# Another list order for a gated linear recurrence with an MLP mixer on one core

## The chip, the core and the metric

The kernel runs on one core of a Trainium2 chip. A core has five engines that run their own queues of instructions in order: PE (TensorE, the matmuls), DVE (VectorE), ACT (ScalarE), POOL (GpSimd) and SP (SyncE, which only issues transfers here). POOL and SP both issue transfers to the DMA engines. The metric is the device time of one execution in microseconds (us). The kernel before takes 167.32 us (median of 3 runs, 167.23 to 168.01).

## The reference

The inputs are q, k, v and f_logit of shape [4, 8, 768, 48] (batch, head, sequence, head width). A gated recurrence runs along the sequence; its output, with the 8 heads side by side as 384 channels, is the x of a mixer: two matmuls across the sequence (768 to 256 to 768) with a residual, then two across the channels (384 to 1536 to 384) with a residual.

```python
f = 1.0 / (1.0 + np.exp(-f_logit))
for t in range(S):
    state = f[:, :, t, :, None] * state + np.einsum('bhd,bhe->bhde', k[:, :, t], v[:, :, t])
    y[:, :, t] = np.einsum('bhd,bhde->bhe', q[:, :, t], state)

xt = x.transpose(0, 2, 1)
h = np.maximum(xt @ w_tok1, 0.0) @ w_tok2
u = x + h.transpose(0, 2, 1)
h2 = np.maximum(u @ w_ch1, 0.0) @ w_ch2
return (u + h2)
```

## The kernel before

The four batches b = 0 to 3 go one after the other, overlapped. A batch is cut into three pairs P = 0 to 2 of 256 positions; a pair is two chunks x = 0, 1 of 128 rows. For each pair the recurrence is done in a blocked form:

- Loads of f, k, q and v (L357), nearly all issued by POOL, to buffers that three batches share. ACT turns f_logit into the negative logarithm of the gate (L454, L457, L459), DVE or POOL adds neighbouring rows (`two`, L448), PE makes running sums with a triangular matrix (L479 for b0, L481 and L482 after it), DVE subtracts (`first`, L499), and ACT takes exponentials into `GG` (L502, L519).
- q and k are multiplied by `GG` into `qk` (L448, one instruction for each j of two, both on DVE except where b0 lets POOL do it), and then turned, so that the head width lies on the partitions. For b0 and b1 PE turns them (L546), and two copies move the result out of PSUM: `kT` (L436 on DVE or L434 on ACT) and the strided `qT`. For b2 and b3 two DMA transposes do it, issued by SP (L531): k straight to `kT`, q to `qJ`, from which POOL (L438) or ACT (L434) makes the strided copy `qT`.
- PE multiplies turned q and k into the scores (L581) and k with v into the parts of the state (L599). DVE masks the scores into `AmT` in four instructions (L624; some of b0's go through ACT and POOL, L619 and L621).
- The state is carried from chunk to chunk by DVE: for b0 it lies in PSUM and is multiplied by the gate of the chunk (L633, the rows `ps<-ps,glast`); later L636, L639 and L641. Each new state is copied to bf16 in two pieces (`state_bd`, L436, L434 or L438).
- PE makes the output of the pair: the earlier state's share (L657) and the masked scores' share (L665). Copies bring it to `x_nat` (fp32) and `x_bf` (bf16).

Then comes the mixer of the batch: tok1 (L709) and its relu `h1T` (L443, L445), tok2 (L725), the residual (L741), its bf16 copy `u_bf`, the turn of `u_bf` to `uT` (by PE for b0 and b1, L766; by two DMA transposes on SP for b2 and b3, L755), ch1 (L784) and its relu `zT` (ACT L443 or DVE L445), ch2 (L803), the last residual (L814) and the store (L702).

All of this is first only a list of operations with their needs. The tuple `ORDER` holds one number for each operation: four times its place in that list, plus which of its allowed engines takes it. `Plan.best` walks `ORDER`, gives each operation a planned start by its own table of costs, deals out the eight PSUM banks as it goes, and at the end sorts all operations by planned start; this is the order in which each engine gets its instructions. Where the plan leaves PE without work for more than 270 ns before 25.5 us, it puts filler matmuls there (L852, function `idle`), whose result nobody reads. The engines take no notice of the planned starts: they run their own queue in order and wait on semaphores.

The lines that choose the engine and place the fillers:

```python
op = self.ops[code // 4]
e = op.engine = op.engines[code % 4]
...
if e == PE and free[PE] < until and t - free[PE] > 270:
    n = int(t / 410) if not free[PE] else int((t - free[PE] - 50) / 215)
    fill = Op((PE,), 0.0, lambda n=n: idle(n), (), (), None, ("fill", n))
```

`idle(n)` issues n // 4 matmuls in fp32 and n % 4 in bf16, each over 512 columns.

Of the kernel before, what the change touches and what calls it, by code (L numbers as in the profile page):

```python
# [35 lines left out]
    884, 888, 920, 1368, 1372, 1264, 164, 168, 172, 1376, 1380, 1156, 1276, 1280, 1284, 1288, 1292, 1240, 1160,
    1400, 1404, 1388, 1384, 1204, 1392, 1208, 1296, 1312, 1412, 1324, 1408, 1300, 1308, 1528, 1304, 1532, 1128,
    956, 932, 1132, 1424, 1416, 924, 908, 936, 1428, 928, 960, 912, 1136, 1316, 1320, 1420, 1140, 1536, 948,
    952, 1540, 1432, 1436, 1440, 1444, 1448, 176, 180, 184, 628, 1396, 1456, 940, 1460, 1328, 945, 1560, 1544,
    1564, 1548, 1552, 2204, 1568, 1468, 1572, 1452, 1088, 1092, 1096, 1340, 1344, 1348, 1100, 1336, 2208, 1332,  # L40
    2228, 1464, 1472, 1584, 1364, 1352, 1588, 1356, 1108, 1576, 1112, 1116, 1580, 1484, 2232, 1592, 1596, 1600,
    1604, 632, 636, 640, 644, 1556, 1476, 1480, 1360, 2212, 1612, 1488, 1620, 1608, 1624, 1616, 1068, 1500,
    1504, 1716, 1720, 1508, 1072, 2236, 1496, 1492, 2216, 1516, 1512, 1640, 1644, 1744, 1628, 1632, 1636, 1648,
    1520, 1652, 2388, 1120, 2240, 2392, 1657, 648, 652, 656, 660, 1748, 1724, 1752, 1728, 1756, 1760, 1660,
    2260, 2248, 2264, 2244, 1764, 1732, 664, 668, 672, 1668, 1524, 2220, 1664, 2252, 1736, 1769, 1741, 2272,
    2268, 1168, 1172, 1772, 1776, 1144, 1104, 2284, 1784, 1788, 1780, 1792, 1796, 1808, 1800, 1804, 1812, 1816,
    2396, 1820, 1824, 1828, 1832, 1836, 1840, 1176, 2280, 1852, 1860, 1856, 1864, 1844, 1848, 1076, 1884, 2400,
    2224, 2408, 2424, 2404, 1888, 1868, 1876, 1892, 1900, 1872, 1880, 2552, 1956, 2412, 1960, 1904, 2420, 2428,
    1897, 1080, 2432, 1180, 2044, 2076, 1988, 2080, 2293, 2048, 1964, 1969, 2556, 2288, 1972, 2012, 2016, 1977,
    1992, 2004, 1908, 1913, 1996, 2008, 2000, 1672, 1676, 2276, 2296, 2300, 2304, 2308, 2312, 2256, 2444, 2436,  # L50
    2416, 2316, 2332, 2560, 2336, 1680, 2340, 1684, 2452, 1688, 1692, 1696, 1700, 2564, 2344, 2320, 2324, 2328,
    2568, 2052, 2056, 2060, 2068, 2036, 1924, 2020, 1916, 1948, 2572, 2584, 2588, 2592, 2596, 2576, 1928, 2072,
    1932, 1921, 2360, 2364, 2025, 2065, 2368, 2028, 1980, 1940, 2348, 1937, 3144, 2033, 2040, 3148, 3168, 1952,
    2376, 2440, 2184, 2188, 2448, 2381, 2385, 3172, 2372, 1944, 1984, 2352, 2356, 2456, 2460, 2464, 2468, 2472,
    3176, 3152, 3184, 2192, 2480, 2488, 3180, 2492, 2484, 2476, 3156, 3188, 3204, 3160, 2496, 2196, 2505, 2501,
    2104, 2608, 3192, 2617, 3200, 3208, 2084, 2108, 2612, 2112, 2116, 2088, 2508, 2512, 2124, 2604, 2092, 2096,
    2524, 2528, 3212, 2600, 2580, 1184, 3196, 2620, 2624, 2628, 2632, 2128, 2532, 1124, 1084, 3224, 3216, 2636,
    2652, 2648, 2640, 2644, 2540, 1704, 2517, 1708, 2521, 2656, 2665, 2536, 3164, 2544, 3492, 3328, 3332, 3496,
    2660, 2548, 2724, 2144, 2728, 2732, 2696, 2736, 2700, 2704, 2668, 2672, 3220, 2676, 2708, 2148, 2680, 2688,
# [826 lines left out]
```

## Time and profile before

| what | value |
|---|---|
| median of 3 runs (lowest, highest) | 167.32 us (167.23, 168.01) |
| the profiled execution's own time | 167.16 us |
| span of the profiled execution, first to last instruction | 165.5 us |
| mean granted TensorE clock | 0.996 |
| busy time PE, DVE, ACT, POOL | 157.5, 128.0, 108.0, 64.7 us |
| filler matmuls L852 | 8.8 us of PE's busy time, before about 25 us |

The profiled execution's time is 1.66 us more than its span; this part lies before the first and behind the last instruction. Busy times of PE count a matmul until its modelled end, so that neighbouring matmuls overlap in the table: the step from one start to the next is what a matmul costs in a full queue. A timeline row gives start, length, engine, line, operation, output and inputs with partitions by elements, the number of instructions in the row, and in brackets the idle time before it with what ended it.

### The profile page before, as it was taken

How to read it: one execution, taken by the hardware profiler on the slowest of the kernel's cores; microseconds unless marked ns; L12 is line 12 of the kernel's file. 1: busy time of each engine (PE TensorE's matmuls, PEld its weight loads, DVE VectorE, ACT ScalarE, POOL GpSimd, SP SyncE). 2: the span in 40 equal slices, each digit the busy share in tenths (PEclk: the TensorE clock that was granted, in tenths of full speed). 3: DMA queues.
4: the chain of work that ended last, by engine and by line, in shares of the span. 5: the costliest groups of instructions: out<-in, count | busy, mean ns of one | idle time of the engine just before them, and what ended most of it. 6: DMA issues, size and time to landing. Idle time of an engine off the chain costs nothing.

```text
span 165.5 us, 4987 instructions
## 1 busy us (share of the span) xinstructions
PE 157.5 (95%) x2050; PEld 100.8 (61%) x2050; DVE 128.0 (77%) x285; ACT 108.0 (65%) x229; POOL 64.7 (39%) x87
## 2 busy tenths in 40 slices
PE   7899998999999999999999999889999999999991
PEld 3286765566665765656666766546657656666561
DVE  6678994998999999999999999937989639271142
ACT  3888985887999999997999567085611422543000
POOL 7998979944876820004603416112122011000000
PEclk9999999999999999999999999999999999999998
DMA  5999999999999999706995991990640043300295
GB/s 121 223 177 171 202 210 241 184 223 210 219 225 222 248 242 210 163 6 128 108 180 135 145 144 34 127 240 1 130 144 6 0 79 80 83 0 0 96 338 190
DMA packets 68184, 24.34 MB, mean 147 GB/s; under 512 B 60897, under 2 KB 67297, under 8 KB 68161
## 3 DMA queue, kind: packets, MB, share of 16 engines
q0 software_dynamic: 41856, 13.77, 68.8%
q1 hardware_dynamic: 25776, 10.06, 29.5%
q8 instruction: 16, 0.26, 0.7%
q10 hardware_dynamic: 528, 0.20, 0.5%
q14 instruction: 8, 0.06, 0.1%
HBM read 25.17 MB, written 4.72 MB: 181 GB/s over the span
## 4 chain that ended last, share of the span: by engine, by line
PE 76%; DMA 4%; ACT 2%; DVE 2%; issue 0%; SPq 0%
PE ps L803 27%; PE ps L784 27%; PE ps L709 5%; DMA uT<-u_bf 4%; PE ps L725 3%; PE ps L665 3%; PE ps L581 3%; PE ps L657 3%; PE ps L546 2%; PE ps L766 1%; PE ps L599 1%; PE ps L481 1%; DVE x_nat L741 1%; DVE x_nat L814 1%; PE ps L482 1%; ACT u_bf L434 1%
## 5 line engine op out<-in xcount | busy, mean ns | idle before, releaser
L803 PE MATMUL ps<-w_ch,zT 128*128 128x384 bf16 (+2 forms) x300 | 52.6, 320 | 0.0
L784 PE MATMUL ps<-uT,w_ch 128*128 128x384 bf16 x288 | 49.6, 326 | 1.5 <-DMA uT<-u_bf 1.4
L784 PEld LDWEIGHTS <-w_ch 128*128 128x128 bf16 x288 | 27.6, 98 | 20.0 <-DMA uT<-u_bf 2.1
L803 PEld LDWEIGHTS <-zT 128*128 128x128 bf16 x300 | 28.0, 98 | 17.0 <-DVE zT L445 0.2
L443 ACT ACTIVATE zT<-ps 128x384 bf16<-128x384 f32 x57 | 25.6, 505 | 18.7 <-PE ps L784 18.4
L624 DVE TENSOR_TENSOR AmT<-ps,mask 128x512 bf16<-128x512 f32 x44 | 28.7, 684 | 1.6 <-PE ps L581 1.5
L445 DVE TENSOR_SCALAR zT<-ps 128x384 bf16<-128x384 f32 x39 | 20.2, 552 | 9.7 <-PE ps L784 6.0
L814 DVE TENSOR_TENSOR x_nat<-x_nat,ps 128x384 f32<-128x384 f32 (+2 forms) x25 | 13.0, 534 | 8.3 <-PE ps L803 8.1
L438 POOL CAST state_bd<-state 48x192 bf16<-48x192 f32 x15 | 5.6, 371 | 24.3 <-DVE state L641 23.6
L438 POOL COPY qT<-qJ 128x1024 bf16<-128x1024 bf16 x3 | 3.5, 1151 | 29.0 <-DMA qJ<-qk 24.6
L448 DVE TENSOR_TENSOR qk<-qk_sb,GG 128x768 bf16<-128x768 bf16 x22 | 12.0, 553 | 1.8 <-ACT GG L519 1.5
L741 DVE TENSOR_TENSOR x_nat<-x_nat,ps 128x384 f32<-128x384 f32 x21 | 10.4, 549 | 3.6 <-PE ps L725 3.6
L357 POOL DMA_DIRECT2D v_sb<-in_v_dram x12 | 10.7, 894 | 5.0 <-DMA w_ch<-in_moe_w_ch_dram 3.8
L519 ACT ACTIVATE GG<-first 128x384 bf16<-128x384 f32 x24 | 12.1, 524 | 0.1
L502 ACT ACTIVATE GG<-ps 128x384 bf16<-128x384 f32 x24 | 11.4, 486 | 0.6 <-PE ps L486 0.5
L434 ACT ACTIVATE x_nat<-ps 128x384 f32<-128x384 f32 x15 | 7.2, 487 | 6.8 <-PE ps L665 6.8
L357 POOL DMA_DIRECT2D qk_sb<-in_k_dram x12 | 10.9, 908 | 1.5 <-POOLq L870 0.8
L357 POOL DMA_DIRECT2D qk_sb<-in_q_dram x12 | 10.8, 900 | 0.8 <-DMA qk_sb<-in_q_dram 0.5
L709 PE MATMUL ps<-x_bf,w_tok 128*128 128x384 bf16 x48 | 10.3, 327 | 0.0
L434 ACT ACTIVATE u_bf<-x_nat 128x384 bf16<-128x384 f32 x13 | 6.3, 533 | 5.8 <-DVE x_nat L741 5.5
L852 PE MATMUL ps<-steady 128*128 128x512 f32 (+1 forms) x18 | 8.8, 595 | 1.0 <-DVE steady L372 1.0
L725 PE MATMUL ps<-h1T,w_tok 128*128 128x384 bf16 x48 | 9.4, 326 | 0.1
(88 smaller groups left out, 233.6 us busy)
## 6 DMA issues: line engine op xcount, KB each, us to landing
out_dram<-x_nat SPq DMA_DIRECT2D x23, 192.0 KB, 2.2
f_sb<-in_f_logit_dram POOLq DMA_DIRECT2D x9, 384.0 KB, 9.4
qk_sb<-in_k_dram POOLq DMA_DIRECT2D x12, 192.0 KB, 8.2
qk_sb<-in_q_dram POOLq DMA_DIRECT2D x12, 192.0 KB, 8.1
v_sb<-in_v_dram POOLq DMA_DIRECT2D x12, 192.0 KB, 8.7
w_ch<-in_moe_w_ch_dram POOLq DMA_DIRECT2D x2, 576.0 KB, 13.7
w_ch<-in_moe_w_ch_dram POOLq DMA_DIRECT2D x1, 1152.0 KB, 10.7
f_sb<-in_f_logit_dram SPq DMA_DIRECT2D x2, 384.0 KB, 5.6
```

Of the source, the lines that this page charges most:

```text
L357: lambda eng=eng, into=held(dst[i], P), of=runs(src, b, P): eng.dma_start(out=into, in_=of),
L434: nc.scalar.activation(out_, in_, AF.Copy, bias=0.0, scale=1.0)
L443: nc.scalar.activation(out_, in_, AF.Relu, bias=0.0, scale=1.0)
L445: nc.vector.tensor_scalar(out_, in_, 0.0, None, ALU.max)
L519: add(ACT, r, lambda n=n: nc.scalar.activation(GG[i][:, 0, n], first[i], AF.Exp, bias=0.0, scale=2.0 * n - 1.0), need=[("first", i)] + ([" ...
L624: add(DVE, r, lambda into=into, made=made, m4=m4: nc.vector.tensor_tensor(into, made(), m4, ALU.mult), need=masks, make=[("AmT", i, js, pa ...
L709: add(PE, rank("tok1", rt), lambda rt=rt, kt=kt, pm=pm: nc.tensor.matmul(banks[pm.at][:, 0:DM], lhsT=w_tok1[:, kt, rt * 128:(rt + 1) * 128 ...
L725: nc.tensor.matmul(banks[pm.at][:, 0:DM], lhsT=w_tok2[:, kt, tt * 128:(tt + 1) * 128], rhs=h1T[:, kt, :], start=(kt == 0 and not held), st ...
L741: nc.vector.tensor_tensor(to, un, banks[pm.at][:, 0:DM], ALU.add)
L784: nc.tensor.matmul(banks[pm.at][:, 0:384], lhsT=w[:, kt, c0:c0 + 128], rhs=uT[:, th, :, kt, :], start=(kt == 0), stop=(kt == 2))
L803: nc.tensor.matmul(banks[pm.at][:, 0:n1 - n0], lhsT=zT[:, kt, tt * 128:(tt + 1) * 128], rhs=w_ch2[:, kt, n0:n1], start=(kt == 0), stop=(kt ...
L814: add(DVE, rank("ch2", tt), lambda un=un, pm=pm, n=n1 - n0: nc.vector.tensor_tensor(un, un, banks[pm.at][:, 0:n], ALU.add), make=[("x_nat" ...
```

## The change

Only the numbers in `ORDER` change. The tuple has 1026 entries before and after, for the same operations, so the loads, matmuls, masks and copies are the same ones; what differs is the order of each engine's queue, which of the allowed engines takes some of the copies and products, the PSUM bank of some results, and the fillers that follow from the plan. The core of the diff, one line of each side:

```diff
@@ -21,61 +21,61 @@
 TURNED = 2
 NQ = 2
 ORDER = (
-    0, 4, 12, 16, 8, 20, 24, 28, 32, 188, 192, 196, 80, 88, 92, 96, 100, 357, 104, 108, 48, 36, 40, 44, 52, 56,
...
+    3780, 3801, 3956, 3884, 3844, 3960, 3817, 3904, 3848, 3785, 3924, 3928, 3864, 3804, 3825, 3932, 3892, 3876,
...
 )
```

Counted over the program, ACT gets 2 more activations (229 for 227), DVE 4 fewer relus (39 for 43), 3 more `state_bd` casts of b0 (5 for 2), 2 more products `qk` of b0 (24 for 22), one more `two` of b0 (12 for 11) and two `qT` copies out of PSUM that ACT had; POOL loses one `two` and two products `qk` of b0, and takes one more `qT` copy of a later batch. There are 5 fillers in fp32 as before, and 16 in bf16 where there were 8. Three places are shown, in the order in which the engines get the instructions. Numbers behind a name are buffers; `ps_4` and the like are PSUM banks; `qk0`, `qk1`, `AmT0`, `AmT1` alternate from pair to pair.

The first place is DVE's queue in the start-up, b0, from the products `qk` of pair 1 (`qk1`) on. Before, it reads:

```order
L448 TENSOR_TENSOR two0_76<-f_sb0_74 128x8x48
L448 TENSOR_TENSOR qk1_85<-qk_sb0_68,GG1_83 128x2x8x48
L633 TENSOR_TENSOR ps_2_123<-ps_2_123,glast0_94 128x192
L624 TENSOR_TENSOR AmT0_92<-ps_4_125,mask_116 128x512
L624 TENSOR_TENSOR AmT0_92<-ps_6_127,mask_116 128x512
L624 TENSOR_TENSOR AmT0_92<-ps_3_124,mask_116 128x512
L633 TENSOR_TENSOR ps_2_123<-ps_2_123,glast0_94 128x192
L499 TENSOR_TENSOR first0_80<-ps_0_121,f_sb0_74 128x384
L436 COPY kT1_89<-ps_4_125 128x1024
L633 TENSOR_TENSOR ps_2_123<-ps_2_123,glast1_95 128x192
L436 CAST state_bd2_103<-ps_2_123 48x4x48 x2
L448 TENSOR_TENSOR qk0_84<-qk_sb0_68,GG0_82 128x2x8x48
```

In the new order the same stretch is:

```order
L448 TENSOR_TENSOR qk1_85<-qk_sb0_68,GG1_83 128x2x8x48 x2
L436 CAST state_bd0_101<-ps_1_122 48x4x48 x2
L448 TENSOR_TENSOR two0_76<-f_sb0_74 128x8x48
L624 TENSOR_TENSOR AmT0_92<-ps_4_125,mask_116 128x512
L633 TENSOR_TENSOR ps_1_122<-ps_1_122,glast0_94 128x192
L624 TENSOR_TENSOR AmT0_92<-ps_3_124,mask_116 128x512
L436 CAST state_bd1_102<-ps_1_122 48x4x48
L624 TENSOR_TENSOR AmT0_92<-ps_6_127,mask_116 128x512
L499 TENSOR_TENSOR first0_80<-ps_5_126,f_sb0_74 128x384
L624 TENSOR_TENSOR AmT1_93<-ps_0_121,mask_116 128x512
L633 TENSOR_TENSOR ps_1_122<-ps_1_122,glast1_95 128x192
L436 CAST state_bd2_103<-ps_1_122 48x4x48 x2
```

Both products `qk` of pair 1 (`qk1`) are now DVE's, and further down both of pair 2 (`qk0`), where POOL had one of each; three more pieces of `state_bd` are DVE's; the copy `kT1` has gone to ACT, and just ahead of this stretch a `qT0` has come.

The second place is the end of the same start-up on DVE, up to the copies `x_bf` that feed tok1 of b0. Before:

```order
L624 TENSOR_TENSOR AmT1_93<-ps_1_122,mask_116 128x512
L436 COPY kT0_88<-ps_6_127 128x1024
L624 TENSOR_TENSOR AmT1_93<-ps_4_125,mask_116 128x512
L633 TENSOR_TENSOR ps_2_123<-ps_2_123,glast2_96 128x192
L624 TENSOR_TENSOR AmT0_92<-ps_0_121,mask_116 128x512
L624 TENSOR_TENSOR AmT0_92<-ps_6_127,mask_116 128x512
L624 TENSOR_TENSOR AmT0_92<-ps_4_125,mask_116 128x512
L436 COPY x_nat0_104<-ps_1_122 128x384
L436 CAST x_bf0_107<-ps_0_121 128x384
```

And in the new order:

```order
L624 TENSOR_TENSOR AmT1_93<-ps_2_123,mask_116 128x512
L436 COPY x_nat0_104<-ps_6_127 128x384
L436 COPY kT0_88<-ps_3_124 128x1024
L436 CAST x_bf0_107<-x_nat0_104 128x384
L624 TENSOR_TENSOR AmT0_92<-ps_0_121,mask_116 128x512
L624 TENSOR_TENSOR AmT0_92<-ps_3_124,mask_116 128x512
L624 TENSOR_TENSOR AmT0_92<-ps_6_127,mask_116 128x512
L633 TENSOR_TENSOR ps_1_122<-ps_1_122,glast2_96 128x192
L436 CAST x_bf0_107<-ps_4_125 128x384
```

The last multiplication of b0's state (`glast2`) stood ahead of the three masks of pair 2, and now stands behind them; `x_nat0`, `kT0` and one `x_bf0` stand ahead of them.

The third place is batch b2, where pair 2's `qk0` must be made before SP can issue its two transposes. On DVE, from the masks of pair 0 (`AmT0`) to these products, before:

```order
L624 TENSOR_TENSOR AmT0_92<-ps_0_121,mask_116 128x512
L636 TENSOR_TENSOR state_99<-ps_7_128,glast0_94 128x192
L499 TENSOR_TENSOR first0_80<-ps_6_127,f_sb0_74 128x384
L639 TENSOR_TENSOR tsum_100<-state_99,ps_3_124 128x192
L624 TENSOR_TENSOR AmT0_92<-ps_5_126,mask_116 128x512
L624 TENSOR_TENSOR AmT0_92<-ps_4_125,mask_116 128x512
L624 TENSOR_TENSOR AmT0_92<-ps_1_122,mask_116 128x512
L448 TENSOR_TENSOR qk0_84<-qk_sb2_70,GG0_82 128x2x8x48 x2
```

In the new order:

```order
L624 TENSOR_TENSOR AmT0_92<-ps_7_128,mask_116 128x512
L624 TENSOR_TENSOR AmT0_92<-ps_5_126,mask_116 128x512
L624 TENSOR_TENSOR AmT0_92<-ps_4_125,mask_116 128x512
L624 TENSOR_TENSOR AmT0_92<-ps_0_121,mask_116 128x512
L499 TENSOR_TENSOR first0_80<-ps_6_127,f_sb0_74 128x384
L814 TENSOR_TENSOR x_nat1_105<-x_nat1_105,ps_3_124 128x384
L448 TENSOR_TENSOR two1_77<-f_sb1_75 128x8x48
L448 TENSOR_TENSOR two0_76<-f_sb1_75 128x8x48
L636 TENSOR_TENSOR state_99<-ps_2_123,glast0_94 128x192
L639 TENSOR_TENSOR tsum_100<-state_99,ps_1_122 128x192
L448 TENSOR_TENSOR qk0_84<-qk_sb2_70,GG0_82 128x2x8x48 x2
```

Two sums `two` and one residual L814 have come in between the masks and the products. POOL's queue beside this, which issues the loads of b3 (buffers `sb0`, and `f_sb1`), read:

```order
L357 DMA f_sb1_75<-in_f_logit_dram 128x8x96
L438 COPY qT1_87<-qJ1_91 128x1024
L357 DMA qk_sb0_68<-in_k_dram 128x8x96
L357 DMA qk_sb0_68<-in_q_dram 128x8x96
L357 DMA v_sb0_71<-in_v_dram 128x8x96
L357 DMA f_sb1_75<-in_f_logit_dram 128x8x96
L438 CAST state_bd2_103<-state_99 48x4x48 x2
L357 DMA qk_sb0_68<-in_k_dram 128x8x96
L438 CAST state_bd0_101<-state_99 48x4x48
L357 DMA qk_sb0_68<-in_q_dram 128x8x96
```

and now reads:

```order
L357 DMA qk_sb0_68<-in_k_dram 128x8x96
L357 DMA qk_sb0_68<-in_q_dram 128x8x96
L438 COPY qT0_86<-qJ0_90 128x1024
L438 COPY qT1_87<-qJ1_91 128x1024
L438 CAST state_bd0_101<-state_99 48x4x48 x2
L357 DMA v_sb0_71<-in_v_dram 128x8x96
L357 DMA f_sb1_75<-in_f_logit_dram 128x8x96
L357 DMA qk_sb0_68<-in_k_dram 128x8x96
L438 CAST state_bd2_103<-state_99 48x4x48
L357 DMA qk_sb0_68<-in_q_dram 128x8x96
L438 CAST state_bd2_103<-state_99 48x4x48
L357 DMA v_sb0_71<-in_v_dram 128x8x96
```

Two loads (k and q of one pair) have moved ahead of the copies `qT`; v, f and k now stand behind the first two casts of b2's `state_bd`, and the last v of b3 follows the last q with one cast between them, where six POOL instructions stood between them before.

108 rows, old and new, of the table ORDER are left out of this document.

## The prediction, on record before the changed kernel ran

> **What bounds the kernel now.** I read the busy times and the chain of the page first, then PE's waits, then timelines of the places where the list differs.
>
> ```profile
> span 165.5 us, 4987 instructions
> PE 157.5 (95%) x2050; PEld 100.8 (61%) x2050; DVE 128.0 (77%) x285; ACT 108.0 (65%) x229; POOL 64.7 (39%) x87
> PE 76%; DMA 4%; ACT 2%; DVE 2%; issue 0%; SPq 0%
> ```
>
> PE is busy for 95% of the span and carries 76% of the chain. The same matmuls run after the change, so the time can move in two ways only: PE waits more or less in the start-up, or it waits more or less in a stall behind it. The waits of PE behind the start-up come down to one row:
>
> ```profile
> PE ps L784 <- DMA uT<-u_bf: 1.4, 2, 0.8
> ```
>
> The columns are total, times and longest: ch1 of b2 waits twice for the transposed `uT`, 1.4 us in all. That is all that a better list could take away in the later part; what a worse one can add has no such limit.
>
> **Term A, the start-up.** Before ch1 of b0 can run, the recurrence of b0 must be through, and DVE is its engine. The first rows are the load of q of pair 1 with its neighbour and their time to landing, then a row by stretch with the busy times of PE, PEld, DVE, ACT and POOL, then DVE's own rows.
>
> ```profile
> L357 POOL DMA_DIRECT2D qk_sb<-in_q_dram x1: 893/893/893, 5.3 to 5.3; - x1
> DMA to landing us min/median/max: 7.6/7.8/7.9
> 13.50:25.04 11.54, 10.61 (x270) 8.16 (x259) 10.84 (x23) 10.08 (x23) 9.94 (x10) 1.00 1.48 197
> 13.51 0.56 DVE L448 TENSOR_TENSOR two<-f_sb 128x384 f32<-128x384 f32 x1 [0.82 <-issue]
> 13.99 0.55 DVE L448 TENSOR_TENSOR qk<-qk_sb,GG 128x768 bf16<-128x768 bf16 x1
> 14.46 0.36 DVE L633 TENSOR_TENSOR ps<-ps,glast 128x192 f32<-128x192 f32 x1
> 14.72 1.88 DVE L624 TENSOR_TENSOR AmT<-ps,mask 128x512 bf16<-128x512 f32 x3
> 16.96 0.56 DVE L499 TENSOR_TENSOR first<-ps,f_sb 128x384 f32<-128x384 f32 x1
> 17.44 0.68 DVE L436 COPY kT<-ps 128x1024 bf16<-128x1024 bf16 x1
> 18.54 0.72 DVE L436 CAST state_bd<-ps 48x192 bf16<-48x192 f32 x2
> 22.47 0.36 DVE L633 TENSOR_TENSOR ps<-ps,glast 128x192 f32<-128x192 f32 x1
> 23.15 1.89 DVE L624 TENSOR_TENSOR AmT<-ps,mask 128x512 bf16<-128x512 f32 x3 [0.33 <-PE ps L581]
> 24.96 0.55 DVE L436 COPY x_nat<-ps 128x384 f32<-128x384 f32 x1
> 25.46 0.56 DVE L436 CAST x_bf<-ps 128x384 bf16<-128x384 f32 x1
> ```
>
> DVE is busy 10.84 of the 11.54 us to the end of the last mask of pair 2 at 25.04: it sets this stretch. From the rows its steps are, start to start or a little more: a product `qk` 0.48, a sum `two` 0.48, a mask 0.60 (three take 1.88), `first` and each 384-wide copy 0.48, `kT` 0.60 like the mask it nearly equals in length, a piece of `state_bd` 0.36, a multiplication of the state 0.36. The work that the new list puts on DVE cannot begin before q of pair 1 has landed, at 5.34 + 7.9 = 13.26 (the row starts at 5.3 in its rounding). From there to the last `glast2` multiplication stand 26 instructions: 4 `qk`, 4 copies and sums of 384 columns (`two`, `first`, `x_nat`, `x_bf`), 5 pieces of `state_bd`, 8 masks, 4 multiplications, 1 `kT`. By the steps: 4 x 0.48 + 4 x 0.48 + 5 x 0.36 + 8 x 0.60 + 4 x 0.36 + 0.60 = 12.48, so DVE is through at 25.74, 0.70 later than 25.04. Its last instruction is now the state's, from which the path runs on through ACT and PE:
>
> ```profile
> 24.18 0.66 ACT L434 ACTIVATE state_bd<-ps 48x192 bf16<-48x192 f32 x2 [0.42 <-PE ps L657]
> 26.03 0.34 PE L657 MATMUL ps<-state_bd,qT 128*128 128x96 bf16 x4
> 27.93 1.79 PE L725 MATMUL ps<-h1T,w_tok 128*128 128x384 bf16 x10
> ```
>
> Two `state_bd` casts on ACT take 0.66, with a wake on each side L657 starts at about 26.55 where it started at 26.03; from there the matmuls are the same down to tok2. So 0.5 later without any idle time on DVE, and 1.2 with the 0.70 of idle that the stretch has now. The program gives a bound further up: it has eight more bf16 fillers of 512 columns. Fillers stand only where the plan sees PE idle, one for each 215 ns by its own rule, so its list leaves PE 8 x 0.215 = 1.7 more without work in the start-up. They delay nothing by themselves, since they stand where PE waits anyway, but they say that the waits are longer. The lower end is 0: a state multiplication steps on by 0.26, not 0.36, where nothing waits for it, and four of these give back 0.4. I take 0.8, between 0.5 and 1.2.
>
> The products that POOL gives up cost it these rows:
>
> ```profile
> 7.10 1.03 POOL L448 TENSOR_TENSOR two<-f_sb 128x384 f32<-128x384 f32 x1
> 14.40 1.64 POOL L448 TENSOR_TENSOR qk<-qk_sb,GG 128x768 bf16<-128x768 bf16 x1
> ```
>
> POOL is freed of 1.03 + 2 x 1.64 = 4.3 us, while DVE pays 3 x 0.48; the 0.48s are in the sum above. POOL's gain is on no path, because what follows it there, the masks of L621, already waits for ACT. The `qT` copies that come to DVE have no row of that form; from below they cost 0.68 as `kT` of the same size, from above the 1.17 that ACT takes for a strided one (row below). Both lie ahead of 13.26, while DVE waits for q, so they cost nothing; without that cover they would add up to 2 x 1.17.
>
> **Term B, the transposes of pair 2 in b2.** SP, POOL, DVE and ACT now, with the landing times of L531 at 80.8 to 82.2, at 92.8 to 94.4, and over the whole program:
>
> ```profile
> 76.16 0.69 DVE L624 TENSOR_TENSOR AmT<-ps,mask 128x512 bf16<-128x512 f32 x1 [0.28 <-PE ps L581]
> 79.59 1.17 DVE L448 TENSOR_TENSOR qk<-qk_sb,GG 128x768 bf16<-128x768 bf16 x2
> 77.65 0.87 POOL L357 DMA_DIRECT2D qk_sb<-in_k_dram  x1
> 80.25 0.92 POOL L357 DMA_DIRECT2D f_sb<-in_f_logit_dram  x1
> 80.80 1.24 SPq L531 DMA_TRANSPOSE qJ<-qk  x1
> 82.13 3.60 SPq L531 DMA_TRANSPOSE kT<-qk  x1
> DMA to landing us min/median/max: 7.4/7.7/7.9
> DMA to landing us min/median/max: 6.8/7.2/7.6
> DMA to landing us min/median/max: 3.0/3.5/7.9
> 89.41 1.17 ACT L434 ACTIVATE qT<-qJ 128x1024 bf16<-128x1024 bf16 x1
> 92.03 0.64 PE L581 MATMUL ps<-qT,kT 48*64 48x128 bf16 x32
> ```
>
> A transpose that has the DMA engines to itself lands 3.0 after its issue, one issued behind loads needs 6.8 to 7.9. In the kernel before, four loads go out from 77.65 to 80.25 just ahead of the pair; it lands late, and nobody waits, because the scores are due 11.2 us after the issue.
>
> In the new list that room is smaller. PE's steps come from the chain:
>
> ```profile
> 84.96 0.57 PE ps L581 x32
> 85.53 0.25 PE ps L599 x32
> 86.22 5.20 PE ps L803 x32
> 91.42 0.17 PE ps L657 x4
> 91.59 0.51 PE ps L665 x32
> ```
>
> A matmul of 384 columns takes 5.20 / 32 = 0.1625. Counted in the new list, PE has 65 of them from the scores of pair 0 to those of pair 2 (32 of L803, 27 of L784, 2 of L709, 4 running sums): 10.56. With two scores at 0.57, two parts at 0.25, two outputs at 0.51 and 12 matmuls of L657 in fours at 0.17 this makes 13.73. In the old list the same count is 80 wide matmuls, and 8 of L657: 16.0. On DVE the road to the transposes is 4 masks 2.40, `first` 0.48, one L814 0.48, two sums `two` 0.96, L636 and L639 at 0.26 each, two `qk` 1.17: 6.0. With 0.5 from the start of the scores to the first mask, SP issues `qJ` 6.55 after the scores of pair 0, which leaves 13.73 - 6.55 = 7.2; less 1.25 for the `qT` copy with its wakes, `qJ` may take 5.95. `kT` goes out 1.33 later (80.80 to 82.13) and needs no copy: 5.9. Ahead of them POOL issues v, f and k, and q and v come just behind.
>
> The landing is the unknown. From below it is 3.0, and there is no stall. From above I take 7.9 and one more load's step of 0.9, 8.8, since two loads follow the transposes: a stall of 2.9. The rows nearest to the case are the four that landed behind loads, 7.9, 7.4, 7.6 and 6.8, mean 7.4: a stall of 7.4 - 5.9 = 1.5, which I take. While ACT's queue stands at that `qT` copy, relus of ch1 wait behind it and hold PSUM banks; between 0 and 0.6, I take 0.2.
>
> **Term C, the uT stall.** The first b2 transposes of `uT` and their landing:
>
> ```profile
> DMA to landing us min/median/max: 3.3/4.7/6.1
> ```
>
> One landed in 3.3, the other in 6.1 beside the load of v. That load now follows q with one cast between and is over long before. So the 1.4 of PE's wait goes: -1.4. If another transfer takes its place nothing is gained, so this term lies between -1.4 and 0; I take -1.4, because POOL's list has no load left then. What is late next is ch1's own bank, which zT frees.
>
> Edits with one answer: relus that go from DVE to ACT, bank numbers, and the order of fillers cost nothing, being covered by PE's full queue behind 25 us (ACT is busy 65%); if ACT were full there, two relus would cost PE up to 1 us. The tail from the last ch2 to the store has the same operations.
>
> **The sum.** 167.16 (span 165.5 and 1.66 around it) + 0.8 + 1.5 + 0.2 - 1.4 = 168.3. The profiled execution is 0.16 below the median of 167.32, so this is +0.6% against the median. Within 0.5% of 167.32, 166.5 to 168.15, is about what a measurement of this kernel can tell from no change.
>
> **Rivals.**
> - *The transposes get their share, and the time is no longer than before (R1).* They stand on SP's queue, the loads on POOL's; if both were served in turn, a transpose would take at most twice the 3.2 that lies between 3.0 and the median 3.5, so 6.4; the stall would be 0.5 and the time 167.16 + 0.8 + 0.5 - 1.4 = 167.1. If both land within 5.9 of their issue it is 166.6, and at 7.2 (a stall of 1.3) the sum passes the 0.5% line. For it speaks that a transpose alone lands in 3.0; against it that the four behind loads took 6.8 to 7.9, over the double. The Trainium skill, page "DMA: Bandwidth & Descriptors", section "Queues, rings and completion order", says that each DMA engine goes round the queue rows that have work, packet by packet; by that rule R1 would hold. The rows agree only in part, since they are longer than a fair share gives.
> - *The loads hold them (R2).* If q and v, issued behind, push the transposes to 8.8, the stall is 2.9 and ACT's queue adds 0.6: 167.16 + 0.8 + 2.9 + 0.6 - 1.4 = 170.1. For it: SP's `kT` at 82.13 took 3.60 for its issue alone, where `qJ` took 1.24, so it was held up there. Against: the old list had four loads just ahead, and still no transpose took over 7.9.
> - *The start-up is no later (R3).* POOL's 4.3 us less could let pair 1 and 2 start sooner, so that DVE's queue begins earlier than 13.26 + waits: A is 0 and the time 167.16 + 1.7 - 1.4 = 167.5. For it: DVE idles 0.70 now; against: that stretch has 23 instructions on DVE now, the new list 26 behind the landing of q, which it cannot move.
>
> **Chances.** The forecast case 0.46 (own range 167.5 to 169.2: 0.28 slower by over 0.5%, 0.18 within), R1 0.20 (0.09 faster, where term A also lies at its low end, 0.11 within), R2 0.22 (slower), R3 0.12 (0.03 faster, 0.07 within, 0.02 slower). Sum: faster 0.12, within 0.5% 0.36, slower 0.52. The range goes from R1's middle, 166.7, to just under R2's, 170.0, leaving about one in ten on each side.
>
> **What the changed profile would show.** A: L657 ahead of tok1 of b0 starts near 26.5 to 26.9, and the first tok2 near 28.7, not 27.93. B: PE's row L581 of pair 2 in b2 waits about 1.5 for `qT` or `kT`, and L531 lands over 6. C: the row `PE ps L784 <- DMA uT<-u_bf` is gone. The prediction is wrong if a wait shows that I have no term for, such as ch2 waiting for `zT` or scores of b1 or b3 waiting for their copies, or if B's landings come within 5.9.

## The result, and the profile after

The changed kernel takes 174.28 us (median of 4 runs, 173.13 to 175.10), the kernel before 167.27 us (median of 4): a ratio of 1.0409 with a 95% interval of 1.0360 to 1.0458. The prediction of 168.3 us (166.7 to 170.0) had the direction and missed the size by 6 us. The profiled execution took 173.54 us. Here and below a ratio and its interval leave out runs more than 1.5% above the fastest of their kernel, while medians and ranges hold every run.

The head of the page of the changed kernel, the chain by engine, and its three longest waits of PE behind the first microseconds:

```profile
span 171.8 us, 5005 instructions
PE 160.6 (93%) x2058; PEld 102.3 (60%) x2058; DVE 129.8 (76%) x285; ACT 108.3 (63%) x231; POOL 61.9 (36%) x85
PE 69%; DMA 8%; ACT 3%; DVE 2%; issue 1%; POOL 1%; DVEq 0%
...
PE ps L581 <- DMA kT<-qk: 3.2, 1, 3.2
PE ps L709 <- POOL AmT L621: 1.2, 1, 1.2
PE ps L665 <- issue: 1.2, 1, 1.2
```

The span is 6.3 us longer. PE's wait for `uT` (1.4 us before) is gone from the list. PE's timeline of the start-up shows two of the new waits:

```profile
14.57 0.64 PE L581 MATMUL ps<-qT,kT 48*64 48x128 bf16 x32
20.99 0.22 PE L665 MATMUL ps<-v_sb,AmT 64*128 64x48 bf16 x3 [1.16 <-issue]
27.04 0.81 PE L709 MATMUL ps<-x_bf,w_tok 128*128 128x384 bf16 x4 [1.25 <-POOL AmT L621]
30.74 1.95 PE L725 MATMUL ps<-h1T,w_tok 128*128 128x384 bf16 x11 [0.25 <-ACT h1T L443]
33.73 2.11 PE L784 MATMUL ps<-uT,w_ch 128*128 128x384 bf16 x12 [0.38 <-ACT uT L434]
```

The first scores of b0 start 1.50 later than before (13.07), tok2 2.81 later (27.93) and ch1 3.05 later (30.68). The third wait is that of b2: the transposes with POOL's loads ahead of them, the landing of the two, and the scores.

```profile
85.36 0.88 POOL L357 DMA_DIRECT2D v_sb<-in_v_dram  x1
87.11 0.89 POOL L357 DMA_DIRECT2D qk_sb<-in_k_dram  x1
85.88 1.25 SPq L531 DMA_TRANSPOSE qJ<-qk  x1
87.22 2.09 SPq L531 DMA_TRANSPOSE kT<-qk  x1
DMA to landing us min/median/max: 6.7/8.0/9.2
96.49 0.64 PE L581 MATMUL ps<-qT,kT 48*64 48x128 bf16 x32 [3.24 <-DMA kT<-qk]
```

Right behind it the granted clock of PE, the third number from the end of a row by stretch, is not 1.00:

```profile
96.00:98.00 2.00, 1.51 (x50) 1.15 (x51) 0.97 (x3) 0.80 (x3) 0.00 (x0) 0.78 1.87 157
98.00:100.00 2.00, 2.00 (x8) 0.97 (x7) 2.00 (x5) 0.49 (x1) 0.00 (x0) 0.50 0.04 3
100.00:102.00 2.00, 2.00 (x29) 1.22 (x28) 1.07 (x3) 1.20 (x3) 0.00 (x0) 0.87 0.10 22
```

At these shares PE loses 2.0 x (0.22 + 0.50 + 0.13) = 1.7 us; at half speed that is a stretch of 3.4 us. So the account of the span is 3.05 (start-up) + 3.24 (wait for `kT`) + 1.7 (clock) - 1.4 (`uT`) = 6.6, against 6.3 measured.

### The profile page after: what moved, and what is told of

The parts are those of the page before. It is cut to its first block, busy times and chain, and to the rows that moved or that the text cites. A ratio compares the mean times of both kernels' runs of the same rounds, so it can differ in the third digit from the quotient of the medians.

```text
span 171.8 us, 5005 instructions
## 1 busy us (share of the span) xinstructions
PE 160.6 (93%) x2058; PEld 102.3 (60%) x2058; DVE 129.8 (76%) x285; ACT 108.3 (63%) x231; POOL 61.9 (36%) x85
## 4 chain that ended last, share of the span: by engine, by line
PE 69%; DMA 8%; ACT 3%; DVE 2%; issue 1%; POOL 1%; DVEq 0%
PE ps L784 25%; PE ps L803 24%; DMA kT<-qk 5%; PE ps L709 5%; PE ps L725 3%; PE ps L581 3%; DMA uT<-u_bf 3%; PE ps L665 2%; PE ps L657 2%; PE ps L546 2%; PE ps L599 1%; ACT u_bf L434 1%; DVE x_nat L741 1%; PE ps L766 1%; DVE qk L448 1%
## 5 line engine op out<-in xcount | busy, mean ns | idle before, releaser
L784 PE MATMUL ps<-uT,w_ch 128*128 128x384 bf16 x288 | 51.7, 329 | 0.6 <-ACT uT L434 0.4
L803 PEld LDWEIGHTS <-zT 128*128 128x128 bf16 x300 | 28.7, 98 | 18.3 <-issue 0.7
L443 ACT ACTIVATE zT<-ps 128x384 bf16<-128x384 f32 x61 | 27.1, 496 | 15.3 <-PE ps L784 15.1
L445 DVE TENSOR_SCALAR zT<-ps 128x384 bf16<-128x384 f32 x35 | 18.5, 552 | 8.2 <-PE ps L784 8.1
L814 DVE TENSOR_TENSOR x_nat<-x_nat,ps 128x384 f32<-128x384 f32 (+2 forms) x25 | 13.1, 534 | 11.2 <-PE ps L803 10.9
L448 DVE TENSOR_TENSOR qk<-qk_sb,GG 128x768 bf16<-128x768 bf16 x24 | 14.2, 615 | 2.3 <-ACT GG L502 1.9
L852 PE MATMUL ps<-steady 128*128 128x512 bf16 (+1 forms) x26 | 11.5, 551 | 1.0 <-DVE steady L372 1.0
L434 ACT ACTIVATE x_bf<-ps 128x384 bf16<-128x384 f32 x13 | 6.2, 488 | 9.5 <-PE ps L665 6.8
L709 PE MATMUL ps<-x_bf,w_tok 128*128 128x384 bf16 x48 | 10.3, 335 | 1.2 <-POOL AmT L621 1.2
L581 PE MATMUL ps<-qT,kT 48*64 48x128 bf16 x384 | 7.7, 219 | 3.4 <-DMA kT<-qk 3.2
L434 ACT ACTIVATE x_nat<-ps 128x384 f32<-128x384 f32 x18 | 8.5, 492 | 2.8 <-PE ps L665 1.5
```

Source lines behind the costliest of these rows:

```text
L434: nc.scalar.activation(out_, in_, AF.Copy, bias=0.0, scale=1.0)
L443: nc.scalar.activation(out_, in_, AF.Relu, bias=0.0, scale=1.0)
L445: nc.vector.tensor_scalar(out_, in_, 0.0, None, ALU.max)
L448: (nc.vector if op.engine == DVE else nc.gpsimd).tensor_tensor(out_, a, b_, what)
L581: nc.tensor.matmul(banks[p_a[js][par].at][half[x], hp * 128:(hp + 1) * 128], lhsT=kT[s][rows, js, hp, half[x]], rhs=qT[s][rows, hp, half[x ...
L709: add(PE, rank("tok1", rt), lambda rt=rt, kt=kt, pm=pm: nc.tensor.matmul(banks[pm.at][:, 0:DM], lhsT=w_tok1[:, kt, rt * 128:(rt + 1) * 128 ...
```

## The experiments

Apart from the loads and fillers named, the engines' queues are those of the lists that they are made from; every list is written out in its file. In these kernels most line numbers are one lower, since the list has a line less, and a few higher behind an edit: L580 and L584 are the scores L581, L664 is L665, L708 is L709, L724 is L725.

**One half of the list each.** Are there two separate losses?

```diff
-ORDER = BEFORE
+ORDER = BEFORE[:191] + (AFTER without the operations of BEFORE[:191])
```

> The list of the kernel before up to the first ch1 of b0, then the changed list for all that is left. Two separate losses (theory): the start-up's 3.05 us (first L784 at 33.73 against 30.68) goes, the stall at the scores of pair 2 in b2 (3.24) and the low clock behind it stay, so 174.3 - 3.0 = 171.2, between 170.3 and 172.0, with the scores' wait still 2 to 4 us. Rival, that the stall in b2 only comes from the late start-up shifting the loads against the transposes: near 167.

```diff
-ORDER = BEFORE
+ORDER = AFTER[:190] + (BEFORE without the operations of AFTER[:190])
```

> The changed list up to the first ch1 of b0, then the list of before for all that is left. Theory: the start-up's loss alone, 167.3 + 3.0 = 170.3, between 169.6 and 171.5, the first L784 near 33.7. Rival, that later slack takes the delay back: 167 to 168.

Measured, beside 166.87 us for the kernel before: 169.80 us (169.66 to 171.87; ratio 1.0202, 1.0138 to 1.0267) and 171.60 us (170.70 to 172.08; ratio 1.0275, 1.0230 to 1.0319). The two differences, 2.9 and 4.7, add up to 7.6, the whole is 7.0. So there are two losses, one in each half of the list, but neither has the size that it has in the whole. The first kernel came out 1.4 lower than forecast, and its profile below shows why for the most part: the wait in b2 is 2.08 there, not 3.24. The second came out 1.3 higher, for a reason that its profile has:

```profile
27.05 1.44 PE L708 MATMUL ps<-x_bf,w_tok 128*128 128x384 bf16 x4 [1.25 <-POOL AmT L620]
27.00:28.00 1.00, 0.95 (x4) 0.48 (x5) 0.27 (x2) 0.65 (x2) 1.00 (x2) 0.50 0.42 152
29.00:30.00 1.00, 1.00 (x31) 0.83 (x31) 0.40 (x1) 0.00 (x0) 1.00 (x2) 0.50 1.61 125
```

The same wait of 1.25 us at the same instruction as in the changed kernel is here followed by a clock of 0.50 from 27 to beyond 30, and the four matmuls behind it take 1.44 instead of 0.81. In the profiled execution of the changed kernel, with the same start, the clock stayed up there. The changed kernel's four times, 173.13 and 173.54, 175.03 and 175.10, lie in two groups 1.7 apart. That would fit a clock that halves here in some executions and not in others, and as well one that stays low longer behind the wait in b2; neither is shown.

The first kernel shows the b2 loss alone:

```profile
92.66 0.64 PE L580 MATMUL ps<-qT,kT 48*64 48x128 bf16 x32 [2.08 <-DMA kT<-qk]
94.00:96.00 2.00, 2.00 (x8) 0.91 (x7) 2.00 (x5) 0.56 (x2) 0.00 (x0) 0.50 0.17 14
DMA to landing us min/median/max: 6.7/7.3/8.0
```

**Where in the program PE's gaps stand.** The gap of 1.16 lies among 32 like matmuls (29, then 3), and the instruction behind it waits for no semaphore. Counted in the trace by matmuls and weight loads in order of start, it stands at row 448; the next wait, ahead of L709, at row 703; and the only such gap of the kernel before, 0.33 at 25.18, at row 701. The distance is 255, and a trace can miss a few records. (The expectations below count some 70 rows less up to there: their places 376 and 632 are these two.) In the trace of the queue that brings instructions there is one piece of 0.02 MB about 2.5 us ahead of each of these three points, and also one ahead of row 445 of the kernel before, where PE did not have to wait. The line is the same for the stretches of 0.25 us from 18.25 and 24.50 in the changed kernel; in the kernel before, from 16.75 and 22.75, the share is 23.4% and 24.4%:

```profile
q8 instruction: 1, 0.02, 22.3%
```

From entering one piece of 256 to the first instruction of the next, PE took 5.9 us (19.24 to 25.18) before, and 6.1 and 6.05 us (about 14.85 to 20.99 to 27.04) after. The theory: a piece is asked for when PE enters the one before, and in the start-up it needs 6 us. (The page shows the DMA engines nearly full then; whether that is why it takes so long, no run tells.) If so, it is the place of an instruction in the program that makes the gap. Two kernels move the places and leave the work:

```diff
     def idle(n):
+        if not padded:
+            padded.append(n)
+            for _ in range(115):
+                nc.tensor.matmul(banks[NBANK - 1][0:64, 0:48], lhsT=steady[0:64].broadcast_to((64, 64)),
+                                 rhs=steady[0:64].broadcast_to((64, 48)), start=True, stop=True)
+            n %= 4
```

> The changed list, with the 3 fp32 fillers of the first group replaced by 115 matmuls of 64x48: the same real work, but all later PE instructions stand about 222 places further down. Theory (PE gets its instructions in pieces of 256, and a piece is not there until about 6 us after PE entered the one before): the pieces now begin near the old places 154, 410 and 666, where PE arrives 6 us or more apart, so the gap of 1.16 within L665 at 21 us is gone, the wait of 1.25 ahead of L709 at 27 us shrinks, and the time falls by 1 to 2 us, to 172.3 to 173.3. Rival (the wait ahead of L709 is for POOL's mask, as the page's releaser has it, and the gap in L665 is something in those matmuls): both gaps stay at the same instructions, time within 0.3 us of 174.3.

The same with 72 in the list of before:

> The list of before, with the 3 fp32 fillers of the first group replaced by 72 matmuls of 64x48, so that later PE instructions stand about 136 places further down. Theory of the pieces of 256: they now begin near the old places 240, 496 and 752, which PE passes at 17.9, 22.7 and 27.9, only 4.8 and 5.2 us apart, so PE stalls about 1.2 us within the scores of pair 2 (old place 496) and up to 0.8 at tok2: 168.3 to 169.3. Rival (places in the program don't matter): 167.3, no new gap.

The kernel before got the gap where it was forecast, within the 32 scores of pair 2:

```profile
23.36 0.30 PE L580 MATMUL ps<-qT,kT 48*64 48x128 bf16 x7 [0.19 <-ACT qT L433]
24.46 0.55 PE L580 MATMUL ps<-qT,kT 48*64 48x128 bf16 x25 [0.81 <-issue]
```

That is row 701 again. It takes 169.21 us (168.07 to 172.16; ratio 1.0115, 1.0062 to 1.0169), within the forecast; but its first scores also begin at 13.80, 0.73 later than in the kernel before, so not all of that is the gap's. In the changed kernel with 115 small matmuls both gaps are gone, the one said to be POOL's mask too, and a new one stands at row 957, again 256 behind 701 (by the count of the expectations near old row 668):

```profile
22.35 0.58 PE L664 MATMUL ps<-v_sb,AmT 64*128 64x48 bf16 x32
27.89 0.81 PE L708 MATMUL ps<-x_bf,w_tok 128*128 128x384 bf16 x4
29.85 0.51 PE L664 MATMUL ps<-v_sb,AmT 64*128 64x48 bf16 x27 [0.42 <-issue]
32.19 1.95 PE L724 MATMUL ps<-h1T,w_tok 128*128 128x384 bf16 x11 [0.25 <-ACT h1T L442]
```

But the time did not fall by the forecast 1 to 2: it is 174.77 us (174.09 to 176.49). The 115 small matmuls took 6.33 us where the fillers took 5.01, the matmuls behind them still ran slowly, and the first scores began at 17.64, 3.07 later than in the changed kernel. By tok2, at 32.19, only 1.45 of this was left: the stretch between is 1.6 shorter without the two gaps. In the profile, of the longest run, that gain was lost again in b2, where PE waited 4.05 for `kT` and the clock was at 0.50 up to 104. So this run shows the places; of the price it shows that it lies between the first scores and tok2.

**The b2 wait: which loads, and what the clock costs.** All on the list with the start of before. Five loads of b3 stand around the two transposes; v, f and k are issued just ahead, q and v behind. Codes 1696 to 1712 are these loads, 2501, 2505 and 2521 are casts of the state on POOL, 2292 is a `qT` copy of b2.

```diff
-    ..., 1708, 2501, 1712, 2521, ...
+    ..., 2501, 2521, 1708, 1712, ...
```

> start_before_rest_after with only the loads of q and v of b3's pair 2 moved on POOL, from just behind the two transposes of b2's pair 2 to behind the next cast of the state, where the transposes are over. If the loads issued behind the transposes hold them, kT lands in 7 or less instead of 8.0, and PE's wait of 2.1 falls to 1 or less: 168.0 to 169.0, lower still if the clock then stays up. If the three loads issued ahead of them do it all, kT lands in 8 as before and the time stays at 169.8.

```diff
-    ..., 1696, 1700, ..., 1704, 2505, ..., 1708, 2501, ..., 1712, ..., 2521, ...
+    ..., 2505, ..., 2501, ..., 2521, 1696, 1700, 1704, 1708, 1712, ...
```

> start_before_rest_after with all five loads (v, f, k, q, v) that stand around these transposes moved behind them. Theory: the transposes land in about 3.2, PE does not wait at the scores of pair 2, the clock stays up: 169.8 - 2.1 - 1.7 = 166.0, between 165.3 and 166.9. Rival, that b3 then lacks its gates or values: a new wait of 1 to 4 us at the scores of b3, 167 to 170.

```diff
-    ..., 2292, ..., 1696, 1700, ..., 1704, 2505, ..., 1708, 2501, ..., 1712, ...
+    ..., 2292, 1696, 1700, 1704, 1708, 1712, ..., 2505, ..., 2501, ...
```

> start_before_rest_after with the same five loads moved up, ahead of the qT copy of pair 1, some 10 us before the transposes of pair 2. Theory: they land before 82, the transposes of pair 2 (issue at 83.2 and 84.6) land in 3 to 4, those of pair 1 land late but have 5 us to spare: 166.0, between 165.3 and 166.9. Rival, that the delay moves to pair 1: a wait at the scores of pair 1, 167 to 169.

```diff
-    ..., 1696, 1700, ..., 1704, 2505, ..., 2521, ...
+    ..., 2505, ..., 2521, 1696, 1700, 1704, ...
```

> start_before_rest_after with only the three loads that stand ahead of the transposes of b2's pair 2 (v, f, k) moved behind them; q and v, issued 2 to 4 us behind the transposes, stay where they are. If the loads ahead make kT late, kT lands in 5 or less, PE does not wait and the clock stays up: 165.5 to 166.6, like rest_after_loads_late. If the loads behind do it, kT still lands in 7 or more and the time is 168 to 170.

The kernel before took 167.13 us beside the first three and 166.77 beside the last.

| kernel | us, median (runs) | ratio to before, 95% interval |
|---|---|---|
| q and v late | 169.28 (167.96 to 172.38) | 1.0109, 1.0045 to 1.0172 |
| all five late | 165.81 (165.63 to 166.00) | 0.9927, 0.9912 to 0.9943 |
| all five early | 169.50 (166.83, 167.61, 171.40, 172.77) | none: times too far apart |
| v, f and k late | 166.15 (165.94 to 166.54) | 0.9965, 0.9948 to 0.9981 |

The landing of the pair of transposes with q and v late (in its run of 172.38 us), and with v, f and k late, and the scores of the latter:

```profile
DMA to landing us min/median/max: 7.3/8.2/9.1
```

```profile
DMA to landing us min/median/max: 3.2/3.2/3.2
90.59 0.64 PE L580 MATMUL ps<-qT,kT 48*64 48x128 bf16 x32
```

So the three loads ahead make the transposes late: with them `kT` lands in 8.0, 9.1 and 9.2 us (start_before_rest_after, q and v late, changed kernel), without them in 3.2. The two behind are not needed for it: with q and v late nothing follows, and `kT` is late all the same. Whether they would delay a transpose is tested less: with v, f and k late, q goes out at 86.61, 1.9 behind `kT`, and v at 88.21, when both transposes have landed. The time with q and v late lies between the two forecasts, and its interval overlaps that of start_before_rest_after (1.0138 to 1.0267), so it does not tell whether these two add to the delay once the transposes are slow. All five early works in two runs of four; the profile, of the run of 167.61, has no wait at these scores, and where the longer two lose their 4 us stays open. All five late beats both kernels, by 1.3 us against the one beside it.

The price of the clock was measured by filling the wait, with 9 filler matmuls ahead of these scores:

```diff
         def scores(js):
+            if b == 2 and P == 2 and js == 0:
+                for _ in range(9):
+                    nc.tensor.matmul(banks[p_a[0][1].at], lhsT=steady.broadcast_to((128, 128)),
+                                     rhs=steady.broadcast_to((128, 512)), start=True, stop=True)
```

> start_before_rest_after with 9 filler matmuls of 512 columns (1.94 us) on PE just ahead of the scores of pair 2 in b2, where PE waits 2.1 us for kT. They do no work that counts and leave the wait as long as it is. If the halved clock behind the wait (0.50 from 94 to 97) costs time of its own, it stays at 1.00 now and the time falls by 1.2 to 1.8, to 168.0 to 168.6. If that clock costs nothing that later slack would not take back, the time stays at 169.8.

It takes 169.70 us (169.13 to 169.88; ratio 1.0154, 1.0132 to 1.0177), no less than the 169.80 without. ACT had still to read the bank, so the fillers came late:

```profile
92.35 2.13 PE L578 MATMUL ps<-steady 128*128 128x512 bf16 x8 [1.66 <-ACT x_nat L433]
94.41 0.64 PE L584 MATMUL ps<-qT,kT 48*64 48x128 bf16 x32
```

The scores started 1.75 later than without fillers (92.66) and the spans are the same 168.1: with the clock at 1.00 throughout, PE made up what the fillers had cost. The second kernel writes to the other bank of the scores, `p_a[0][0]` for `p_a[0][1]`:

> rest_after_filled with the 9 fillers written to the other bank of these scores, which is free by then, so that they run from the begin of PE's wait (about 90.5) and end before kT lands at 92.6. If the halved clock behind the wait costs time of its own, the scores begin as early as in start_before_rest_after, the clock stays at 1.00 and the time is 167.8 to 168.6. If not, 169.6 to 169.9.

Now the fillers start at 90.98, and the rest of the wait is

```profile
93.57 0.64 PE L584 MATMUL ps<-qT,kT 48*64 48x128 bf16 x32 [0.47 <-DMA kT<-qk]
```

at a clock of 1.00. The time is 168.82 us (168.04 to 170.13; ratio 1.0120, 1.0065 to 1.0175), a little above the forecast 167.8 to 168.6; the interval overlaps that without fillers, so the times alone don't price the clock. The profiles do. The same instruction behind the scores, in start_before_rest_after and with fillers in the first and the second bank:

```profile
98.88 0.33 PE L656 MATMUL ps<-state_bd,qT 128*128 128x96 bf16 x4
98.95 0.33 PE L660 MATMUL ps<-state_bd,qT 128*128 128x96 bf16 x4
98.11 0.33 PE L660 MATMUL ps<-state_bd,qT 128*128 128x96 bf16 x4
```

From the start of the scores to it, PE takes 6.22 us with the clock halved, and 4.54 (98.95 - 94.41 and 98.11 - 93.57) with the clock up. With v, f and k late it takes 4.55 (90.59 to 95.14). So the halved clock costs 1.68 us, and later slack does not give it back: behind this point the distance between the kernels changes by less than 0.2 up to the last matmul. In the profile of q and v late, behind a wait of 3.70, the clock stays at 0.50 until 100, and the same stretch takes 7.22 (94.26 to 101.48): 2.7 us more than with the clock up.

**The start-up's loss, with the b2 wait gone.** The changed list with all five loads late, then two versions of it.

> The changed list with only the five loads (v, f, k, q, v of b3) moved behind the transposes of b2's pair 2. If the two losses add up, the stall and its clock go and the start-up's stays: 174.3 - 4.0 = 170.3, between 169.5 and 171.5, and the wait for kT is gone. Rival, that the two losses hang together: below 169 or above 172.

The first filler group's bf16 one replaced by small ones, the fp32 ones kept:

```diff
     def idle(n):
+        if not padded:
+            padded.append(n)
+            for _ in range(18):
+                nc.tensor.matmul(banks[NBANK - 1][0:64, 0:48], lhsT=steady[0:64].broadcast_to((64, 64)),
+                                 rhs=steady[0:64].broadcast_to((64, 48)), start=True, stop=True)
+            n -= n % 4
```

> after_loads_late with the one bf16 filler of the first group replaced by 18 matmuls of 64x48, so that later PE instructions stand 34 places further down, while the fp32 fillers that keep PE busy stay. Theory of the pieces of 256: they begin near the old places 86, 342 and 598; PE enters the first at about 13 instead of 14.8, the next is there at 19.2, before PE arrives at 19.6, so the gap of 1.2 within L665 is gone; a gap of up to 0.6 is left at about 25 within L599, in place of the one of 1.25 ahead of L709. Time 1.0 to 1.8 below after_loads_late. Rival (the order of the work alone makes the start-up late): within 0.3 of after_loads_late.

```diff
     def idle(n):
+        if n == 11:
+            n = 8
```

> after_loads_late with the group of 2 fp32 and 3 bf16 fillers ahead of the first scores (12.05 to 14.64) cut to the 2 fp32 ones. In the changed kernel kT and qT were there at 13.97, and the scores began at 14.57, when the fillers were through. Theory: the scores begin 0.5 earlier and with them the first piece of instructions, so the time falls by 0.4 to 0.6. Rival (fillers only fill waits and delay nothing): no change, within 0.2.

The changed list with late loads takes 170.29 us (167.51, 170.20, 170.39, 170.95). The median is the forecast one by luck: three times lie 3 us above the fourth, and the profile of the longest has a loss that the forecast did not have. PE waited 1.59 us for DVE before 11.46, with the clock halved behind that:

```profile
11.46 0.62 PE L545 MATMUL ps<-ident,qk 128*128 128x128 bf16 x8 [1.59 <-DVE qk L447]
12.00:14.00 2.00, 2.00 (x27) 1.21 (x25) 0.57 (x3) 1.96 (x5) 1.33 (x2) 0.52 2.01 171
14.00:16.00 2.00, 2.00 (x7) 1.12 (x5) 1.61 (x3) 1.72 (x3) 0.76 (x1) 0.63 2.01 171
```

Why DVE was late there stays open. The wait for `kT` is gone as forecast, and with it more than the forecast 4.0: 3.24 and 1.7 are 4.9. With 18 small matmuls it takes 167.84 us (167.22 to 168.30; ratio to before 1.0048, 1.0018 to 1.0078), with the shorter filler group 167.51 us (166.59 to 167.93; 1.0036, 1.0011 to 1.0061). Both are steady, and both are 2.5 to 2.8 below that median but no lower than its one quick run; the times alone do not settle the prices. The timelines do more. PE with the 18:

```profile
15.50 0.64 PE L580 MATMUL ps<-qT,kT 48*64 48x128 bf16 x32
20.22 0.58 PE L664 MATMUL ps<-v_sb,AmT 64*128 64x48 bf16 x32
26.16 0.43 PE L598 MATMUL ps<-v_sb,qk 64*64 64x48 bf16 x16 [1.04 <-ACT x_nat L433]
30.46 1.95 PE L724 MATMUL ps<-h1T,w_tok 128*128 128x384 bf16 x11 [0.25 <-ACT h1T L442]
```

and with the shorter group:

```profile
13.94 0.64 PE L580 MATMUL ps<-qT,kT 48*64 48x128 bf16 x32
19.99 0.82 PE L853 MATMUL ps<-steady 128*128 128x512 bf16 x3 [0.56 <-issue]
25.98 0.48 PE L708 MATMUL ps<-x_bf,w_tok 128*128 128x384 bf16 x2 [0.79 <-issue]
29.36 1.95 PE L724 MATMUL ps<-h1T,w_tok 128*128 128x384 bf16 x11 [0.25 <-ACT h1T L442]
```

Each gap is where the pieces of 256 put it: with the 18 the first is gone and the next stands ahead of L599, at row 703; with the shorter group, 6 instructions less, the gaps have moved by some instructions, out of L665 and into the midst of L709, and stand at rows 447 and 701. So in every kernel these gaps stand at the same rows to within three, whatever instruction is there. (The page puts the gap ahead of L599 down to ACT's `x_nat`, which ends at 25.99; in this one run the two causes fall together.) The run with the shorter group also settles the wait ahead of L709, which the page put down to POOL's mask: two matmuls run, then the gap comes, with no releaser.

From the first scores to tok2 it takes 14.86 us before, 16.17 in the changed kernel, 14.96 with the 18, 15.42 with the shorter group and 14.55 with the 115. The gaps in it sum to 2.4 in the changed kernel, and to 1.0, 1.35 and 0.4 in the other three: each us of gap taken away took 0.7 to 0.9 off the stretch. (The scores of the 18 and the 115 start later than those of the changed kernel, by 0.93 and 3.07, so some of this may be DVE and the loads being further.) Against the kernel before the stretch is 1.3 longer, and that is no more than these gaps make. The other 1.5 is that the first scores start late. The overlong filler group made 0.6 of it (13.94 against 14.57). For the rest there is a row in each profile: `kT` of pair 0, which DVE copied from 11.76 on (first row, before), is now ACT's, which comes to it 1.2 later (second row, after).

```profile
11.76 0.69 DVE L436 COPY kT<-ps 128x1024 bf16<-128x1024 bf16 x1 [0.33 <-PE ps L546]
12.96 1.01 ACT L434 ACTIVATE kT<-ps 128x1024 bf16<-128x1024 bf16 x1
```

ACT is through at 13.97, where DVE was at 12.45; with the shorter group the scores begin as soon as this copy is over. No run gives the copy back to DVE, so this part is read from the rows and not tested.

DVE in its turn waits for PE: its longest wait in the start-up of the changed kernel, from 21.56 on, comes just behind PE's gap of 1.16.

```profile
22.38 0.37 DVE L633 TENSOR_TENSOR ps<-ps,glast 128x192 f32<-128x192 f32 x1 [0.82 <-PE ps L599]
```

## Why the prediction was wrong

- **Term C, the `uT` stall (-1.4): right.** The wait row is gone, and the transposes of b2 landed in 4.6 or less.
- **Term A, the start-up (+0.8, upper end 1.7): the place right, the size wrong.** Tok2 came 2.81 later, at 30.74 and not near 28.7, and ch1 3.05. Three steps failed. The sentence that fillers "delay nothing by themselves, since they stand where PE waits anyway" was wrong: the group at 12.05 ran to 14.64, the scores began at 14.57, and the shorter group let them begin 0.6 earlier. The `qT` copies ahead of 13.26 were said to "cost nothing" because DVE waits for q then; but PE waits for what is copied there, and `kT`, whose move to ACT no term had, was there 1.5 later. And DVE's queue was not the bound all the way: its 26 instructions start at 13.46, near the 13.26 reckoned, but end at 27.27, not 25.74. Their steps were summed rightly (13.81 less 1.44 of idle time is 12.37, forecast 12.48); the idle time, taken as 0 to 0.70, was not. The longest piece of it, 0.82, is a wait for PE just behind PE's gap of 1.16. The profile before had such a gap only as "0.33 <-issue", which was not followed up. R3, that the start-up is no later, fell.
- **Term B, the transposes (+1.5, upper end 2.9): the reckoning of the room right, the landing wrong.** The wait should be the landing less the room of 5.9: 9.2 - 5.9 = 3.3, measured 3.24. The landing was taken as 7.4 from four rows; it was 6.7 for `qJ` and 9.2 for `kT`, and over the assumed end of 8.8. With the start of before, in the same place of the same list, it was 8.0. The three loads just ahead are the cause, as the runs with v, f and k late show. Why the landing was 8.0 to 9.2, when the kernel before shows 7.4 and 7.9 behind four loads, stays open. R2's reason, the two loads issued behind, was not it: that R2's number came nearest is luck.
- **R1 fell.** The Trainium skill, page "DMA: Bandwidth & Descriptors", section "Queues, rings and completion order", has an engine go round its queues packet by packet. The prediction read that as equal shares of time, which gave its estimate of 6.4, twice the 3.2 alone. The traces show 6.7 to 9.2 with loads ahead and 3.2 without: a fair share of time is not what a transpose gets here.
- **What no term had: the clock behind a wait.** The prediction priced a wait of PE at its length, and put 0.2 behind it for ACT's queue. Behind the wait of 3.24 the clock was low for some 3.4 us, worth 1.7 by the rows by stretch, and the filled runs give 1.68 for such a stretch. The profile before could not show it, with no wait over 0.8 behind the start. The Trainium skill, page "TensorE: Matmul & The Clock Gate", section "HAM oscillation — how this bites in real kernels", gives the rule of no idle gaps over about 3.4 us. The traces agree that the clock halves, and differ in the bound: it also halved at waits of 1.25 us (at 27.05), 1.59 (at 11.46) and 2.08 (at 92.66). It stayed up at waits of 1.25 (changed kernel, at 27.04), 1.52 (changed list with late loads, at 29.60) and 1.66 (first filled kernel). So a wait of 1.25 to 1.66 does it in one execution and not in another; all those from 2.08 on did it.

With the sizes of the profiled execution in its own sum, 167.16 + 3.05 + 3.24 + 1.7 - 1.4 = 173.75, against 173.54 for the profiled execution. One term (the clock) was missing, and two were less than half of what they are.

## What to carry to other kernels

A transpose by DMA that something waits for should not be issued right behind large loads: moving three loads behind it took 3.7 us off a list (169.80 to 166.15; 2.1 of wait and 1.7 of clock), and moving all five made it 0.7% faster than the kernel before. Price a wait of PE of 2 us or more in the middle of a kernel like this at its length plus 1.7 to 2.7 us for the clock behind it, and one of 1.25 to 1.66 at its length plus nothing to 1.7. An "issue" gap within a run of like matmuls is worth locating by its row in the queue: if gaps stand 256 rows apart, and stay at these rows when the work is moved, the order of the work is not what makes them. Fillers are not free either: they take up rows, and a group that is too long holds up what comes behind it.

## What the runs showed of the hardware

PE gets its instructions in pieces of 256 (16 pieces of 0.02 MB for its some 4,100 instructions). In the start-up, where loads keep the DMA engines nearly full, a piece is there only about 6.0 us after PE has entered the one before: 5.9, 6.1 and 6.05 us in these two kernels, 5.6 to 6.3 in the other runs with such gaps. A stretch of 256 short instructions that would run in less has a gap, and fillers, two instructions for 215 ns each, use up places. The Trainium skill, page "Runtime: NRT & Kernel Launch", section "Instruction fetch mechanics", tells of blocks of 16 KiB, 256 instructions, and calls the cost of a boundary mostly hidden; the size agrees, and in this start-up the cost is 0.3 to 1.3 us at a boundary. A releaser that the page names for such a wait (POOL's mask ahead of L709) can be one that only happened to end in time.
